# A new order of all steps in a sketched linear attention followed by a gated feed-forward layer

## The chip, the cores and the metric

The kernel runs on one core of a Trainium2 chip. A core has five engines with instruction streams of their own: TensorE (PE in the profile, its weight loads PEld), VectorE (DVE), ScalarE (ACT), GpSimd (POOL) and SyncE (SP, which here only issues transfers). Each engine runs its stream strictly in the order in which the program was written; an instruction that has to wait holds up everything behind it on its engine. The metric is the device time of one execution in microseconds.

## The reference

For 4 batches and 4 heads, 1088 tokens of 32 features each, queries and keys are turned into 64 products of two 8-wide projections; attention is linear in them. The result, laid out as 4352 tokens by 128, goes through a feed-forward layer of 2048 hidden units with a Swish whose slope is given for each unit.

```python
def phi(x):                                   # r = 8
    a = np.einsum('rd,bhsd->bhsr', S1, x)
    b = np.einsum('rd,bhsd->bhsr', S2, x)
    return np.einsum('bhsi,bhsj->bhsij', a, b).reshape(*x.shape[:-1], r * r)
q_p, k_p = (phi(q), phi(k))
kv = np.einsum('bhsf,bhsd->bhfd', k_p, v)
z = np.sum(k_p, axis=2)
num = np.einsum('bhsf,bhfd->bhsd', q_p, kv)
den = np.einsum('bhsf,bhf->bhs', q_p, z)[..., None] + 1e-06
x = (num / den)                               # then to (4352, 128)
h = x @ w_in
g = h * (1.0 / (1.0 + np.exp(-beta * h)))
return (g @ w_out).astype(np.float32)
```

## The kernel before

There is one list of short names, `SEQ`, and the program is written by calling the step of each name in turn. No scheduler reorders anything: the list is the order on every engine, and also the order in which buffers are handed out. A buffer that is used again makes its next writer wait for its last reader.

**The feed-forward part.** The tokens are cut into 9 chunks, eight of 512 and one of 256. A chunk has eight waves (the last has four). `W` (`first`, L433) is a wave's two matmuls of 512 columns (four of 256 in the last chunk) from xT, the attention's result, into a `wave` tile of PSUM; `G` (`silu`, L449) is one ScalarE instruction over the wave's 1024 columns; `V` (`second`, L400) is the wave's two matmuls into the output's accumulator; `E` (`put_out`, L414) transposes a finished chunk on VectorE and stores it. There are 68 waves, and two `wave` tiles. The scaled weights are made in the kernel: `up`/`uv` make 256 columns of winp on GpSimd or VectorE (L342), `wa`/`wp` make woutp on ScalarE or GpSimd (L351, L358). The slope beta is split in three bf16 parts (`bsv` on VectorE or `bsp` on GpSimd, L319 to L322), broadcast by TensorE (`be0`, `be1`, L327) and copied out by ScalarE (`bc0` to `bc3`, L337).

**The attention part, for a batch b.** `lk`, `lq`, `lv` issue its loads on SyncE. `tk`, `tq` transpose keys and queries on VectorE (L457, L463). `kp` projects the keys on TensorE (L475), `ka` transposes that on VectorE into kab (L489), and `op`/`ov` form products of the two projections, a piece at a time, on GpSimd or VectorE (L512, tile kp). `v` multiplies them with v on TensorE (L536). `z` sums the products on VectorE (L523), `zm` and `wz` carry the sums on into the tile sw. For batches 0 and 1 a shorter way takes their place: `gr` (L714, tile gram), `gd` (L734), `wm` (L760) and `wc` (L769). `qp` projects the queries together with the denominators (L596), `qa` transposes the two halves of the result (L608), `dp`, `di` and `as` form the denominators' reciprocals and scale one factor (L616, L626/L629, L634), `yp`/`yv` form the queries' products (L512, tile qo), `t` transposes them (L639, tile qt). `kd`, `np`, `nc` turn the key-value sums (L574, L577, L586, tile nd), `n` is the numerator on TensorE (L652), and `xa`/`xv` copy it to xT (L664).

**Batch 0's first 512 tokens** go a way of their own, so that the first waves can start early: `aA`, `bA`, `cA`, `mA` make their query products, `dA` and `iA` their denominators (iA: L786, L788, L789, L791 on VectorE), `kd0`, `nd0`, `nc0`, `nA` the numerator, and `xA` writes xT (L825 on VectorE).

**Buffers that matter here.** PSUM has two `wave` tiles (also used by `qp` and `n`), one `two` tile (`be`, `kp`, `qp`, `nd0`, `n` by turns) and one `one` tile (`gr`, `wm`, `np`, `v` of batches 1 to 3 and others by turns). The tiles kp, qo, qab and qt have one buffer each.

**Warming matmuls.** `h` is one matmul of 400 columns on constant data (L196) with no use for the result; it keeps TensorE busy. Six are issued ahead of the list.

SyncE's transfers use eight semaphores in turn, so that a transfer is issued only when the eighth before it has landed.

Of the kernel before, what the change touches and what calls it, by code (L numbers as in the profile page):

```python
# [18 lines left out]
SEQ = """
    lqA lq0 h li0 h li1 h lk1 sp lv0 bsv h h s0 h sw h s1 tk0b be0 sk h tk0a h bc0 h li2 h h bc1 tqA  # L20
    h sr lo1 kp0 tq0 src up0 h lk2 ka0a bA up1 ka0b aA ca0a lo0 ov04 gr0 op02 cA0 ov03 ov00 h op01 h
    be1 ztv op06 gdv0 lq1 tk1 bc2 h op05 h lv1 h ca0b zm cA1 op08 h mA0 bc3 h op07 v03 v05 mA1 wm0
    kp1 zc up3 wc0 v01 rb dA ka1 up2 v02 h h iA lo2 up7 v07 v08 v00 wa6 wa7 v04 up5 qp0 lq2 wa4 wa5
    v06 gr1 qa00 kd0 op13 kda0 qa01 nd0 h gdv1 h tk2 nc0 h lv3 h nA wa2 wa3 dpp0 wm1 h op10 wc1 h xA
    wa0 wa1 np0 h di0 nca0 W op12 W tq1 G kp2 asp0 h G W ov11 h v12 uv4 lo3 G W yv00 v13 G lv2 W ka2
    yp01 h v10 t00 G v11 qp1 up6 t01 kda1 W op22 wa10 wa11 qa11 h G V qa10 op23 lk3 W np1 lq3 tq2 n0
    G dpp1 ncv1 W ov21 xa01 V xa00 op20 di1 G W V G asp1 z20 W V wp4 G W yp13 V G W z21 v23 G W yp12
    v22 G W yp10 v21 t13 zm2 G W wz2 V yp11 G t10 W v20 t12 wa12 wa13 wp7 qp2 t11 G V qa20 V kda2
    qa21 n1 E0 dpv2 V di2 xa10 V W xv11 asp2 V G tk3 W yp22 V G W tq3 kp3 G W yv21 V G W yp20 ka3 V
    G W yp23 t20 V G V W E1 np2 op32 W G t21 V ncv2 V G ov31 W V op33 t22 G W t23 V G W op30 V G W  # L30
    v33 z30 G W V G n2 z31 v31 xa21 W V G W xv20 zm3 v30 G W wz3 V G qp3 E2 v32 qa31 W V qa30 G W V
    dpv3 G W di3 V G kdv3 W asp3 V G yp31 W V G W yp32 V G W yv33 V G V yp30 W E3 np3 W G t31 V ncv3
    V G t32 W V t30 G W t33 V G W V G V W V G W V G n3 E4 W xa31 V G xv30 W V G V W V G W V G W V G
    W V G W V G W E5 V G W V G W V G V W V G W V G W V G W V G W E6 V G W V G W V G W V G W V G W V
    G W V G V W E7 V G V V V E8
"""


# [919 lines left out]
```

## Time and profile before

| | before |
|---|---|
| median of 3 runs | 104.11 us (103.93 to 106.35) |
| the profiled execution's own time | 103.7 us |
| its span, first to last instruction | 101.9 us |
| PE, ACT, DVE, POOL busy | 96.3, 79.1, 64.0, 41.0 us |
| granted TensorE clock | 0.992 |
| first wave's matmuls start | 19.55 us |
| batch 3's numerator (last attention work on PE) | 73.96 to 75.50 us |
| last matmul of the chain ends | 98.1 us |
| DMA | 11.35 MB; the 16 engines are full until about 20 us |

The times in rows of the trace are microseconds from the span's start: a start, a duration, the engine, the line, the operation, output and input tiles, the number of instructions merged, and in brackets how long the engine had been idle and for whom. "x4" rows give the time from the first's start to the last's end.

### The profile page before, as it was taken

To read this page: it belongs to the slowest core of one execution; us is meant where nothing else is said; L and a number is where in the kernel's file an instruction comes from. 1 tells how busy PE (TensorE), PEld (TensorE's weight loads), DVE (VectorE), ACT (ScalarE), POOL (GpSimd) and SP (SyncE) were. 2 spreads that over 40 slices of the span, in tenths; PEclk is the share of its full clock that TensorE was granted. 3 is DMA by queue.
4 is the path that set the end of the run, shared out by engine and by line. 5 is a ranking of instruction groups with operands and counts; after the bars stand their busy time and mean duration, and the time that the engine had idled before them with its cause. 6 is when DMAs were issued, how large, how long until landed. Compare 5 with 4: busy or idle time off the path is not lost.

```text
span 101.9 us, 2974 instructions
## 1 busy us (share of the span) xinstructions
PE 96.3 (95%) x1225; PEld 48.4 (47%) x1225; DVE 64.0 (63%) x105; ACT 79.1 (78%) x110; POOL 41.0 (40%) x60
## 2 busy tenths in 40 slices
PE   5999999998999999999999999999999999999940
PEld 2465556435353454434544544454454444446730
DVE  2389989999999999995999578358032020020210
ACT  1553618699589995599997859999969999999920
POOL 7306998993976980499800001960000000000000
PEclk9999999999999999999999999999999999999996
DMA  1999999954738100330320000506012306014054
GB/s 29 306 264 385 415 398 378 358 176 149 214 71 330 68 6 0 60 52 0 57 46 6 0 9 10 90 0 103 0 19 31 60 6 100 0 24 71 8 88 67
DMA packets 23576, 11.35 MB, mean 111 GB/s; under 512 B 19323, under 2 KB 21387, under 8 KB 23563
## 3 DMA queue, kind: packets, MB, share of 16 engines
q1 hardware_dynamic: 22419, 11.08, 39.2%
q10 hardware_dynamic: 1144, 0.09, 0.8%
q8 instruction: 9, 0.15, 0.6%
q14 instruction: 4, 0.03, 0.1%
HBM read 8.94 MB, written 2.23 MB: 110 GB/s over the span
## 4 chain that ended last, share of the span: by engine, by line
PE 88%; DVE 7%; issue 0%
PE wave L433 30%; PE moeout L400 29%; PE kvz L196 8%; PE nps L652 6%; PE kvz L536 4%; PE qps L596 3%; PE kps L475 2%; DVE qo L512 1%; DVE winp L342 1%; DVE qT L463 1%; PE aps L684 1%; PE ndps L577 1%; DVE kp L512 1%; DVE kab L489 1%; PE gram L714 1%; PE kvz L714 1%
## 5 line engine op out<-in xcount | busy, mean ns | idle before, releaser
L449 ACT ACTIVATE g<-wave 128x1024 f16<-128x1024 f32 x68 | 64.8, 1036 | 4.8 <-PE wave L433 4.7
L433 PE MATMUL wave<-xT,winp 128*128 128x512 f16 (+1 forms) x144 | 40.6, 369 | 0.0
L400 PE MATMUL moeout<-g,woutp 128*128 128x512 f16 (+1 forms) x144 | 38.4, 367 | 0.1
L433 PEld LDWEIGHTS <-winp 128*128 128x128 f16 x144 | 15.2, 115 | 15.4 <-issue 5.3
L414 DVE STREAM_TRANSPOSE o_sb<-moeout 128x512 f32<-128x512 f32 (+1 forms) x9 | 6.1, 683 | 26.1 <-PE moeout L400 26.1
L400 PEld LDWEIGHTS <-woutp 128*128 128x128 f16 x144 | 13.8, 97 | 14.8 <-issue 0.8
L512 POOL TENSOR_TENSOR kp<-kab 128x256 f32<-128x256 f32 (+2 forms) x15 | 14.3, 976 | 1.9 <-DVE kab L489 1.6
L512 POOL TENSOR_TENSOR qo<-qab 128x512 f32<-128x512 f32 (+1 forms) x11 | 13.9, 1295 | 0.2
L196 PE MATMUL kvz<-idle 128*128 128x400 f16 x40 | 10.8, 381 | 1.2 <-DVE idle L115 1.1
L639 DVE STREAM_TRANSPOSE qt<-qo 128x512 f32<-128x512 f32 (+1 forms) x14 | 10.1, 753 | 0.0
L634 POOL TENSOR_TENSOR qab<-qab,rc 128x288 f32<-128x288 f32 (+1 forms) x4 | 2.5, 632 | 18.7 <-DVE rc L629 18.7
L523 DVE TENSOR_REDUCE zs<-kp 128x128 f32<-128x1152 f32 x4 | 8.4, 2145 | 0.0
L536 PEld LDWEIGHTS kvz<-kp,v 128*32 128x32 f32 x288 | 4.9, 109 | 5.7 <-issue 3.9
L536 PE MATMUL kvz<-kp,v 128*32 128x64 f32 x288 | 7.3, 224 | 0.0
L342 POOL TENSOR_TENSOR winp<-w_in_sb,beta_bc 128x256 f16<-128x256 f32 x7 | 5.1, 753 | 5.2 <-DMA w_in_sb<-in_moe_w_in_dram 5.2
L196 PEld LDWEIGHTS <-idle 128*128 128x128 f16 x40 | 3.8, 109 | 4.7 <-issue 2.5
L652 PE MATMUL nps<-qt,nd 32*32 32x288 f32 (+1 forms) x256 | 6.0, 386 | 0.0
L664 ACT CAST xT<-nps 128x576 f16<-128x576 f32 (+1 forms) x5 | 2.8, 553 | 3.7 <-PE nps L652 3.6
L463 DVE STREAM_TRANSPOSE qT<-q 128x1088 f32<-128x1088 f32 (+2 forms) x5 | 5.2, 1047 | 0.4 <-DMA q<-in_q_dram 0.4
L457 DVE STREAM_TRANSPOSE kT<-k 128x1088 f32<-128x1088 f32 (+2 forms) x5 | 5.4, 1074 | 0.0
L608 DVE STREAM_TRANSPOSE qab<-qps 128x576 f32<-128x576 f32 (+1 forms) x8 | 5.2, 683 | 0.3 <-PE qps L596 0.2
L351 ACT ACTIVATE woutp<-w_out_sb,rbeta 128x128 f16<-128x128 f32 x12 | 4.1, 396 | 1.6 <-DMA w_out_sb<-in_moe_w_out_dram 1.6
(102 smaller groups left out, 71.1 us busy)
## 6 DMA issues: line engine op xcount, KB each, us to landing
v<-in_v_dram SPq DMA_DIRECT2D x15, 144.0 KB, 5.7
k<-in_k_dram SPq DMA_DIRECT2D x3, 544.0 KB, 6.5
q<-in_q_dram SPq DMA_DIRECT2D x3, 544.0 KB, 7.5
out_dram<-o_sb SPq DMA_DIRECT2D x20, 64.0 KB, 2.0
w_out_sb<-in_moe_w_out_dram SPq DMA_DIRECT2D x4, 256.0 KB, 6.6
w_in_sb<-in_moe_w_in_dram SPq DMA_DIRECT2D x2, 256.0 KB
w_in_sb<-in_moe_w_in_dram SPq DMA_DIRECT2D x1, 512.0 KB
k<-in_k_dram SPq DMA_DIRECT2D x1, 288.0 KB, 2.8
```

The source lines that it names most:

```text
L196: nc.tensor.matmul(out=kvz0[:, HC : HC + 400], lhsT=idle, rhs=cut(idle, [[0, 25], [1, 16]]), start=fresh, stop=True, skip_group_check=True,)
L342: eng.tensor_tensor(out=winp[:, c0:c1], in0=w_in_sb[:, c0:c1], in1=beta_bc[:, c0:c1], op=MUL)
L400: nc.tensor.matmul(out=moe["acc"][:, :tw], lhsT=woutp[:, j, :], rhs=g[jj], start=(j == 0), stop=(j == NJ - 1),)
L414: nc.vector.transpose(out=o_sb[:, :nt, :].rearrange("p t d -> p (t d)"), in_=PS["acc", ci][:, :tw])
L433: nc.tensor.matmul(out=wv[:, jj // per, o : o + tw], lhsT=cut(winp, [[step, P]], c), rhs=xT[:, t0 : t0 + tw], start=True, stop=True,)
L449: nc.scalar.activation(out=g, in_=wv, func=ACTF.Silu)
L463: nc.vector.transpose(out=qT2[b % 2][:, t0:t1].rearrange("p t s -> p (t s)"), in_=q_t[b][:, t0:t1].rearrange("p t d -> p (t d)"),)
L512: eng.tensor_tensor(out=cut(dst[b][:, j0:j1], [[F, n], [R, R], [1, R]]), in0=left, in1=cut(a0, [[w, n], [0, R], [1, R]], o + R), op=MUL,)
L523: nc.vector.tensor_reduce(out=RB["zs", b][:, hs].rearrange("p h f -> p (h f)"), in_=KP[b][:, :, hs].rearrange("p j h f -> p (h f) j"), axi ...
L536: nc.tensor.matmul(out=KVZ[b][32 * h : 32 * h + 32, :F], lhsT=v_t[b][:, h, j, :], rhs=KP[b][:, j, h, :], start=(b > 0 and summed[b] == 0), ...
L639: nc.vector.transpose(out=QT[b][:, j0:j1].rearrange("p j h c s -> p (j h c s)"), in_=QO[b][:, j0:j1].rearrange("p j h f -> p (j h f)"),)
L652: nc.tensor.matmul(out=ts[g // 2][32 * h : 32 * h + 32, g % 2, : 32 * nq], lhsT=ND[b][rows, fc, 32 * h : 32 * h + 32], rhs=QT[b][rows, :nq ...
```

## The change

Only the list `SEQ` differs: 473 names in place of 474. The same work is done. Two warming matmuls fall away (32 `h` in place of 34). Some steps change the engine: the split of beta goes from VectorE to GpSimd; the denominators' products go from GpSimd to VectorE for batches 0 and 1 and from VectorE to GpSimd for batches 2 and 3; the scaling for batch 3 goes to VectorE; all of batch 0's query products are on GpSimd; batch 3 has two pieces of key products and two of query products on VectorE in place of one each; ScalarE takes two more pieces of woutp (14 in place of 12) and one more copy each to nd and xT. All else is order. The first two lines of the list, as an example:

```diff
-    lqA lq0 h li0 h li1 h lk1 sp lv0 bsv h h s0 h sw h s1 tk0b be0 sk h tk0a h bc0 h li2 h h bc1 tqA
-    h sr lo1 kp0 tq0 src up0 h lk2 ka0a bA up1 ka0b aA ca0a lo0 ov04 gr0 op02 cA0 ov03 ov00 h op01 h
+    lqA lk1 h lv0 h h h sp tk0a h bsp h h h li1 tk0b h lq0 sk li0 s1 kp0 s0 sw lk2 sr ka0b h h src
+    ka0a h op07 ca0b h h tqA ca0a be0 op06 ov04 lo1 gr0 bc0 op01 li2 rb aA bc1 ov05 lo0 op00 bA ztv
...
```

On VectorE, from the transposed key projections of batch 1 (kab) to the first write of xT, the order was this (dps, rc and rb are the denominators of the first 512 tokens, qab the query projections of batch 0, gd a part of batch 1's gram matrix, kT batch 2's keys):

```order
L489 STREAM_TRANSPOSE kab<-kps 128x2x9x32 [waits PE_49]
L786 STREAM_TRANSPOSE dps<-dps 128x256 [waits DVE_49,PE_49,Activation_49]
L788 TENSOR_SCALAR rc_355<-dps 128x16 [waits DVE_49]
L789 RECIPROCAL rc_355<-rc_355 128x16 [waits DVE_49]
L791 STREAM_TRANSPOSE rb<-rc_355 128x512 [waits DVE_49]
L608 STREAM_TRANSPOSE qab<-qps 128x2x5x32 [waits PE_49] x2
L734 TENSOR_TENSOR gd_429<-gram,mh 128x32 [waits PE_49]
L457 STREAM_TRANSPOSE kT_112<-k 128x1088 [waits DMAHW1_49]
L825 TENSOR_TENSOR xT<-nps,rb 128x512 [waits DVE_49,PE_49]
```

On the same engine, between the same two steps, it is now:

```order
L489 STREAM_TRANSPOSE kab<-kps 128x2x9x32 [waits PE_49]
L457 STREAM_TRANSPOSE kT_112<-k 128x1088 [waits DMAHW7_49]
L512 TENSOR_TENSOR kp<-kab 128x512 [waits DVE_49,PE_49,Pool_49]
L608 STREAM_TRANSPOSE qab<-qps 128x2x5x32 [waits PE_49]
L786 STREAM_TRANSPOSE dps<-dps 128x256 [waits PE_49,Activation_49]
L788 TENSOR_SCALAR rc_403<-dps 128x16 [waits DVE_49]
L789 RECIPROCAL rc_403<-rc_403 128x16 [waits DVE_49]
L791 STREAM_TRANSPOSE rb<-rc_403 128x512 [waits DVE_49]
L608 STREAM_TRANSPOSE qab<-qps 128x2x5x32
L825 TENSOR_TENSOR xT<-nps,rb 128x512 [waits DVE_49,PE_49]
```

Batch 2's keys, a piece of batch 1's key products and half of qab now stand ahead of the denominators, and gd no longer stands here.

On ScalarE, around the first waves, the order was this (nd is batch 0's turned key-value sums, g a wave's result; the numbers tell the buffers apart):

```order
L769 COPY sw1_117<-w_457 128x8 [waits PE_49]
L351 ACTIVATE woutp_148<-w_out_sb_90,rbeta_149 128x128 x2
L586 COPY nd_476<-ndps_469 128x256 [waits PE_49]
L449 ACTIVATE g_486<-wave_478 128x1024 [waits PE_49]
L449 ACTIVATE g_499<-wave_482 128x1024 [waits PE_49]
```

On ScalarE, at the same place, it is now:

```order
L351 ACTIVATE woutp_148<-w_out_sb_90,rbeta_149 128x128 x3
L449 ACTIVATE g_460<-wave_449 128x1024 [waits PE_49]
L586 COPY nd_463<-ndps_444 128x256
L449 ACTIVATE g_465<-wave_457 128x1024 [waits PE_49]
L449 ACTIVATE g_489<-wave_479 128x1024 [waits PE_49]
L449 ACTIVATE g_516<-wave_486 128x1024 [waits PE_49]
L769 COPY sw1_117<-w_511 128x8 [waits PE_49]
```

The copy to nd, which empties the `one` tile, has moved behind the first wave's silu, and the copy to sw1 behind the fourth. On TensorE the gram matrix of batch 1 (`gr1`, which writes the `one` tile next) has moved from ahead of the first wave to behind the second; then come two waves, batch 2's key projections, `wm1`, and two more waves.

On VectorE, behind the first write of xT, the order was this (dpr feeds batch 0's denominators, qT are the transposed queries of batches 1 and 2):

```order
L626 TENSOR_REDUCE rc<-dpr_114 128x20 [waits Pool_49]
L629 RECIPROCAL rc<-rc 128x20 [waits DVE_49]
L463 STREAM_TRANSPOSE qT_115<-q 128x1088 [waits DMAHW3_49]
L512 TENSOR_TENSOR kp<-kab 128x512
L342 TENSOR_TENSOR winp<-w_in_sb,beta_bc 128x256 [waits DMAHW7_49]
L512 TENSOR_TENSOR qo<-qab 128x768 [waits Pool_49]
L489 STREAM_TRANSPOSE kab<-kps 128x2x9x32 [waits PE_49]
```

On the same engine and at the same place, it is now:

```order
L616 TENSOR_TENSOR dpr_114<-qab 128x20x8 [waits DVE_49]
L342 TENSOR_TENSOR winp<-w_in_sb,beta_bc 128x256 [waits DMAHW1_49]
L626 TENSOR_REDUCE rc<-dpr_114 128x20 [waits DVE_49]
L629 RECIPROCAL rc<-rc 128x20 [waits DVE_49]
L463 STREAM_TRANSPOSE qT_111<-q 128x1088 [waits DMAHW3_49]
L463 STREAM_TRANSPOSE qT_115<-q 128x1088 [waits DMAHW4_49]
L734 TENSOR_TENSOR gd_491<-gram,mh 128x32 [waits PE_49]
L489 STREAM_TRANSPOSE kab<-kps 128x2x9x32 [waits PE_49]
```

Both batches' queries are now transposed ahead of gd and of batch 2's kab, and the products of keys and of queries that stood here are on GpSimd or further ahead. From batch 3's numerator to the end the two lists name the same steps with the same number of waves left: 22 `W`, 22 `G`, 28 `V`.

More of the change, by code (lines that the diff above doesn't have):

```diff
@@ L19 @@
 SEQ = """
-    lqA lq0 h li0 h li1 h lk1 sp lv0 bsv h h s0 h sw h s1 tk0b be0 sk h tk0a h bc0 h li2 h h bc1 tqA
-    h sr lo1 kp0 tq0 src up0 h lk2 ka0a bA up1 ka0b aA ca0a lo0 ov04 gr0 op02 cA0 ov03 ov00 h op01 h
-    be1 ztv op06 gdv0 lq1 tk1 bc2 h op05 h lv1 h ca0b zm cA1 op08 h mA0 bc3 h op07 v03 v05 mA1 wm0
-    kp1 zc up3 wc0 v01 rb dA ka1 up2 v02 h h iA lo2 up7 v07 v08 v00 wa6 wa7 v04 up5 qp0 lq2 wa4 wa5
-    v06 gr1 qa00 kd0 op13 kda0 qa01 nd0 h gdv1 h tk2 nc0 h lv3 h nA wa2 wa3 dpp0 wm1 h op10 wc1 h xA
@@ L25 @@
[L25 to L34, printed above, removed]
@@ L35 @@
-    G W V G V W E7 V G V V V E8
+    lqA lk1 h lv0 h h h sp tk0a h bsp h h h li1 tk0b h lq0 sk li0 s1 kp0 s0 sw lk2 sr ka0b h h src
+    ka0a h op07 ca0b h h tqA ca0a be0 op06 ov04 lo1 gr0 bc0 op01 li2 rb aA bc1 ov05 lo0 op00 bA ztv
+    lq2 tk1 op03 h cA1 v00 lq1 h be1 cA0 up2 mA1 lo3 h v03 bc2 op08 h v04 mA0 bc3 h lv1 up3 ov02 kp1
+    gdv0 up1 tq0 v08 v02 v06 v01 ka1 wm0 h wc0 v05 zm tk2 h v07 kd0 ov10 zc qp0 kda0 dA up0 qa00 iA
+    nd0 h h lo2 nc0 h wa4 wa5 h h nA wa2 wa3 lv2 qa01 h h wa0 wa1 xA h h np0 dpv0 h W uv5 op13 di0 W
@@ new lines @@
+    G tq2 nca0 G op12 gr1 tq1 W up7 h lq3 W G gdv1 up6 kp2 lv3 wm1 G up4 ka2 op11 W wc1 W G V asp0
+    v13 yp01 G lk3 qp1 v10 wa8 wa9 v11 yp00 t01 V wa6 wa7 V W v12 qa11 G qa10 wa14 wa15 t00 kda1
+    wa10 wa11 dpv1 n0 ov21 di1 op20 W xa01 V xa00 op22 G np1 V W op23 nca1 W G V wp6 G z20 asp1 V V
+    yp10 W W z21 G v20 yp13 v23 G W v22 G yp12 t10 zm2 W E0 G yp11 t13 V V wz2 W t12 qp2 G t11 V
+    qa20 v21 V qa21 n1 dpp2 di2 W xa11 V xa10 kdv2 V asp2 tk3 G W V G np2 yv22 W V yp20 G W E1 kp3 G
+    yp21 t22 W ka3 V G yp23 W t21 G t20 W V op31 G t23 W V G ncv2 op32 W V G W ov30 V ov33 G W V G
@@ L36 @@
+    z31 V W V G W v33 z30 G v30 v31 W n2 G E2 zm3 tq3 W xa21 V G W wz3 V G xv20 W V G W V G qp3 v32
+    qa31 W kda3 V qa30 G W V dpp3 G W V di3 G W asv3 V G W yp33 E3 np3 G W V G yv30 W V yv32 G W
+    yp31 t33 V G W V t31 G W t32 V G t30 W V ncv3 G W V G W V G n3 E4 W xa31 V G xv30 W V G V W V G
+    W V G W V G W V G W V G W E5 V G W V G W V G V W V G W V G W V G W V G W E6 V G W V G W V G W V
+    G W V G W V G V W V G W E7 V G V V V E8
 """
```

## The prediction

> **What bounds the kernel now.** First the busy times and the chain that ended last, then the stages, then single rows.
>
> ```profile
> PE 96.3 (95%) x1225; PEld 48.4 (47%) x1225; DVE 64.0 (63%) x105; ACT 79.1 (78%) x110; POOL 41.0 (40%) x60
> PE wave L433 30%; PE moeout L400 29%; PE kvz L196 8%; PE nps L652 6%; PE kvz L536 4%; PE qps L596 3%; PE kps L475 2%; DVE qo L512 1%; DVE winp L342 1%; DVE qT L463 1%; PE aps L684 1%; PE ndps L577 1%; DVE kp L512 1%; DVE kab L489 1%; PE gram L714 1%; PE kvz L714 1%
> L196 PE MATMUL kvz<-idle 128*128 128x400 f16 x40 | 10.8, 381 | 1.2 <-DVE idle L115 1.1
> ```
>
> TensorE is the bound, and 8% of the chain is warming matmuls: filler, which marks where TensorE waits for others. The stages, cut at the first wave and at the ends of the numerators (columns: stretch, length, then busy PE, PEld, DVE, ACT, POOL, the clock, DMA):
>
> ```profile
> 19.55:29.31 9.76, 9.22 (x208) 4.39 (x207) 9.73 (x13) 8.21 (x12) 7.85 (x9) 1.00 0.55 172
> 29.31:41.18 11.87, 11.85 (x209) 5.28 (x210) 11.59 (x17) 10.17 (x14) 6.98 (x8) 1.00 0.30 98
> 41.18:56.15 14.97, 14.97 (x164) 7.05 (x168) 13.72 (x16) 13.02 (x14) 8.25 (x7) 1.00 0.24 38
> 56.15:75.56 19.41, 19.41 (x225) 9.33 (x226) 10.86 (x19) 16.81 (x18) 4.58 (x4) 1.00 0.18 28
> 75.56:98.13 22.57, 22.53 (x117) 11.89 (x116) 2.91 (x5) 21.20 (x23) 0.00 (x0) 1.00 0.25 39
> ```
>
> Until 41 us **VectorE is as full as TensorE** (9.73 of 9.76, 11.59 of 11.87), so what is put ahead of a critical step there delays it by its full length. From 41 to 75 us TensorE has no gap. In the tail ScalarE is nearly full too: 21.20 of 22.57.
>
> So the test of a new order is this: at equal TensorE work done (so many waves, `V`s and attention steps), is the clock earlier or later than before? I add it up at three points, from rows of before. A wave's two matmuls, and a `V`'s, count 0.43 us there, as in this piece of the chain:
>
> ```profile
> 42.15 0.43 PE wave L433 x2
> ```
>
> **The first wave.** It needs the first write of xT, on VectorE.
>
> ```profile
> 12.15 0.60 ACT L337 COPY beta_bc<-betaps 128x512 f32<-128x512 f32 x1
> 13.95 0.78 DVE L489 STREAM_TRANSPOSE kab<-kps 128x576 f32<-128x576 f32 x1 [0.33 <-PE kps L475]
> 14.65 0.46 DVE L786 STREAM_TRANSPOSE dps<-dps 128x256 f32<-128x256 f32 x1
> 16.28 0.87 DVE L608 STREAM_TRANSPOSE qab<-qps 128x320 f32<-128x320 f32 x2
> 17.26 1.30 DVE L457 STREAM_TRANSPOSE kT<-k 128x1088 f32<-128x1088 f32 x1
> 18.75 0.69 DVE L825 TENSOR_TENSOR xT<-nps,rb 128x512 f16<-128x512 f32 x1 [0.19 <-PE nps L814]
> 19.36 0.33 DVE L626 TENSOR_REDUCE rc<-dpr 128x20 f32<-128x180 f32 x1
> 21.09 0.82 DVE L512 TENSOR_TENSOR kp<-kab 128x512 f32<-128x512 f32 x1
> 21.84 1.28 DVE L342 TENSOR_TENSOR winp<-w_in_sb,beta_bc 128x256 f16<-128x256 f32 x1
> ```
>
> Before, xT waited 0.19 us for TensorE. Now VectorE does kab, kT, kp, half of qab, the denominators, the other half, xT. By starts to next starts: 0.70 + 1.25 + 0.75 + 1.63 + 0.87 = 5.20 us (kT's 1.30 less 0.05 of overlap). Batch 0's keys are projected earlier now, because the split of beta has left VectorE. But batch 1's projections still wait for the last copy of beta, since both use the tile `two`, and I leave kab at 13.95. xT then starts at 19.15, and the first wave at about 19.95: **0.4 us later**. (TensorE's own way there, from half of qab over nd0, nc0 and nA past the `h`s, ends at about the same time.) What was gained on the keys is hidden.
>
> The keys and queries must also have landed. Each transfer waits for the eighth before it, so an issue dates a landing:
>
> ```profile
> 8.50 0.33 SPq L172 DMA_DIRECT2D w_out_sb<-in_moe_w_out_dram  x1
> 10.69 0.33 SPq L172 DMA_DIRECT2D w_out_sb<-in_moe_w_out_dram  x1
> 15.24 0.33 SPq L172 DMA_DIRECT2D w_out_sb<-in_moe_w_out_dram  x1
> 16.60 0.33 SPq L122 DMA_DIRECT2D q<-in_q_dram  x1
> ```
>
> The transfers eight ahead of these end 1344, 2144, 3488 and 4032 KB of the old queue. In the new one batch 2's keys end 3264 KB, so about 14.5 us, and their transpose starts at 14.65: just in time. Batch 2's and 1's queries end 4832 and 5376 KB; at the 319 KB/us between the second and the last row that is 19.1 and 20.8 us, and their transposes start after 21.5.
>
> **From there to batch 0's numerator.**
>
> ```profile
> 19.55 1.03 PE L433 MATMUL wave<-xT,winp 128*128 128x512 f16 x4
> 20.51 0.71 PE L475 MATMUL kps<-kT,sk 64*32 64x288 f32 x16
> 19.58 0.37 ACT L586 COPY nd<-ndps 128x256 f32<-128x256 f32 x1
> 20.18 4.92 ACT L449 ACTIVATE g<-wave 128x1024 f16<-128x1024 f32 x5 [0.23 <-PE wave L433]
> 19.91 1.25 DVE L463 STREAM_TRANSPOSE qT<-q 128x1088 f32<-128x1088 f32 x1
> 26.61 1.40 DVE L608 STREAM_TRANSPOSE qab<-qps 128x576 f32<-128x576 f32 x2
> 28.13 1.17 PE L652 MATMUL nps<-qt,nd 32*32 32x160 f32 x64
> ```
>
> TensorE has two waves issued 0.96 us after the first starts (19.55 to 20.51). Then `gr1` needs the tile `one`, which ScalarE's copy to nd empties, and this copy is now behind a silu: the silu starts 0.63 us after the first wave (20.18), 0.96 us on the next thing can start (4.92 us for five), and the copy takes 0.37. So TensorE **stands about 1.0 us**, from 20.9 to 21.9. What is queued behind: gram, all waves, batch 2's keys. The gram and `wm1` (0.8 us) were done before the first wave in the old order, while four `h`s that ran behind it are gone (about 0.8 us in all). Then TensorE has gram to 22.6, two waves and an `h` to 23.7, batch 2's projections to 24.35, and `wm1`, which needs gd. VectorE reaches gd behind xT, the denominators' product (0.3, an estimate from its size beside the reduce), winp (1.2), reduce and reciprocal (0.55) and two transposes of queries (1.25 each): 19.76 + 4.55 = 24.3. So wm1 loses only a little, to 24.5. After it come two waves, a `V`, kv products and the query projections of batch 1, to 27.0. The numerator needs their two transposes (1.40) and that of 768 columns of batch 0's products (0.9, an estimate by the row at 35.29, quoted below): 29.3, while TensorE has work until 28.85. It ends at 30.4. Before, it ended at 29.31 with the same 7 waves, but one `V` in place of three and batch 1's ndps (0.22) done already. At equal work: 30.4 - 0.86 + 0.22 - 29.31 = **0.45 us late**. "Four waves ahead of its queries" thus fills time that the order itself opens.
>
> **To batch 1's numerator.** VectorE sums batch 2's key products, which GpSimd makes.
>
> ```profile
> L512 POOL TENSOR_TENSOR kp<-kab 128x512 f32<-128x512 f32 x6 | 6.4, 1068 | 1.6 <-DVE kab L489 1.6
> L512 POOL TENSOR_TENSOR kp<-kab 128x768 f32<-128x768 f32 x3 | 4.5, 1509 | 0.3 <-POOL winp L342 0.3
> 31.18 4.21 DVE L523 TENSOR_REDUCE zs<-kp 128x128 f32<-128x1152 f32 x2
> 35.29 0.98 DVE L639 STREAM_TRANSPOSE qt<-qo 128x768 f32<-128x768 f32 x1
> 36.65 1.89 DVE L639 STREAM_TRANSPOSE qt<-qo 128x512 f32<-128x512 f32 x3
> 38.72 1.45 DVE L608 STREAM_TRANSPOSE qab<-qps 128x576 f32<-128x576 f32 x2 [0.18 <-PE qps L596]
> 39.58 1.60 PE L652 MATMUL nps<-qt,nd 32*32 32x288 f32 x64
> ```
>
> The tile kp is free when batch 1's last kv product is done, at 28.85. Three pieces (1.07 + 1.07 + 1.51) end at 32.5, the two sums at 36.8. Then VectorE has four transposes of qt, one output of the same size as qt's of 512 (0.6), the two small steps of `wz` (0.4, between the rows at 35.29 and 36.65) and qab: 0.96 + 1.89 + 0.6 + 0.4 + 1.4 = 5.2 us, so 42.0. TensorE runs out of `V`s at 41.4, stands 0.6 us, and ends the numerator at 43.5 with 15 waves and 12 `V`s; before 41.18, with 16 and 8. 43.5 - 3 x 0.43 - 41.18 = **1.0 us late**.
>
> **The rest.** The order is nearly the old one, and VectorE has room again. ScalarE has one more xT copy there (about 0.64) and kvd (0.37), and fewer finished waves in store at 43.5 us (3 for 8), so that TensorE waits for it more often. From nothing to those 1.0 us; I take 0.2, because ScalarE had 1.95 us idle in that stage and 2.6 in the next. The tail has the same steps. What hides the two more woutp pieces (0.35 each) on ScalarE is its wait for TensorE before batch 0's numerator; without that they push the eighth silu back by 0.7.
>
> **Sum.** 0.45 + 0.55 + 0.2 = 1.2 us. The profiled execution took 103.7, the median of the runs is 104.11; on the median, **105.3 us** (+1.2%).
>
> **The shared port.** Products on VectorE and GpSimd at once:
>
> ```profile
> 49.68 1.39 DVE L512 TENSOR_TENSOR kp<-kab 128x512 f32<-128x512 f32 x1
> 46.96 3.56 POOL L512 TENSOR_TENSOR kp<-kab 128x512 f32<-128x512 f32 x3
> 44.98 0.65 DVE L512 TENSOR_TENSOR qo<-qab 128x512 f32<-128x512 f32 x1
> 42.95 4.05 POOL L512 TENSOR_TENSOR qo<-qab 128x512 f32<-128x512 f32 x3
> ```
>
> The same size took VectorE 1.39 us, 0.82 and 0.65, the last beside GpSimd for its whole length. The Trainium skill, "GPSIMD Engine Reference", section "Key points", says that GpSimd shares its SBUF interfaces with VectorE and contends with its instructions of two SBUF inputs. By that rule each such pair is slow; the trace bears it out in the first row and not in the third.
>
> **Rivals.** (1) *Slower by more*: the new order puts the product on kab and GpSimd's 768-column piece of the same batch side by side ahead of the first wave, as both start when batch 0's kv is done. At 1.39 in place of 0.75 the first wave loses 0.6 more, and the pieces of batch 2 ahead of the sums as much again; with 0.3 for a late landing of batch 2's keys, 106.8 us. For it speaks the full VectorE, against it the 0.65. Chance 0.17. (2) *No effect*: TensorE's work is fixed, and the waits replace filler: the stand of 1.0 us is paid by the four `h`s, VectorE's order is made good by waves done ahead. 104.1, chance 0.15. (3) *Not slower*: if batch 1's projections start at once after the last copy of beta (12.75 before) with kab at 13.4, and TensorE's way to nA runs early because the keys are early, the first wave comes at 19.4 to 19.5, batch 0's numerator is level, and the sums of batch 2 start early enough that TensorE never stands at batch 1's: then the 1.0 us of the two stands turns into filler saved, 103.1. It decides at the start of VectorE's kab: before about 13.4 it is this case. Chance 0.15. That the waves aren't ahead at all, because winp's pieces are late on GpSimd (1.51 + 1.07 and three pieces of winp at no more than 1.28 each, from batch 0's last kv product at about 15, end by 21.4; the wave comes at 24.5), is within (1).
>
> **How the numbers follow.** The forecast has 0.53, for 104.5 to 106.1. The range 103.2 to 107.1 leaves out about half of (3) and a third of (1). 2% is about what a measurement of this kernel can tell from no change: 102.0 and 106.2 are its bounds. Faster takes a little of (3), 0.03; slower most of (1) and the forecast's upper edge, 0.19; the rest, 0.78, is within.
>
> **What would show it.** First wave near 19.95 with VectorE, not nps, ending last before it; TensorE idle near 1 us behind the second wave, released by the nd copy; batch 0's numerator waiting for qt or qab; batch 1's end near 43.5 behind zs; from batch 3's numerator on the same distances. If the first wave is ahead of 19.5 or the sums of batch 2 start before 32, I am wrong towards (3).

## The result, and the profile after

The changed kernel takes **107.4 us** (106.68 to 107.81 in four runs), the kernel before 104.4 beside it: 1.030 times, interval 1.021 to 1.038. The forecast was 105.3 with a range to 107.1: the direction was right, the loss 3.0 us in place of 1.2. The profiled execution took 107.16 us, with a span of 105.4. Executions that were disturbed are left out of all ratios and of the run times in the table below; the profiled executions of e4, e8, e9, e13, e17 and e19 are among them, and of these only the distances behind the first wave are compared.

The busy times of the changed kernel, and its stages, cut at the same events as before (first wave, ends of the four numerators, end of the last matmul):

```profile
PE 97.7 (93%) x1223; PEld 48.7 (46%) x1223; DVE 63.8 (61%) x101; ACT 79.9 (76%) x114; POOL 41.3 (39%) x61
...
19.91:31.31 11.40, 10.03 (x233) 5.14 (x232) 8.92 (x14) 9.14 (x17) 6.83 (x9) 1.00 0.68 224
31.31:44.95 13.64, 12.71 (x214) 5.78 (x214) 11.04 (x15) 9.28 (x14) 9.51 (x9) 1.00 0.15 28
44.95:60.62 15.67, 15.42 (x195) 7.31 (x198) 15.11 (x17) 14.46 (x16) 6.75 (x6) 1.00 0.12 20
60.62:79.06 18.44, 18.33 (x190) 8.50 (x190) 11.12 (x17) 16.80 (x19) 3.78 (x3) 1.00 0.18 29
79.06:101.58 22.52, 22.52 (x117) 11.90 (x116) 2.91 (x4) 21.20 (x23) 0.00 (x0) 1.00 0.25 39
```

The clock is 1.00 in all five stretches, as it was before, so nothing of the loss behind the first wave is the clock's. TensorE stands 1.37 and 0.93 us in the first two of these stretches (10.03 busy of 11.40, 12.71 of 13.64), where it stood 0.54 and 0.02 before, and VectorE, once full there, waits too: at times each waits for the other, as the brackets below show. The tail is as long as before.

Single rows of the timeline of the changed kernel, in the order of time:

```profile
13.73 0.74 DVE L489 STREAM_TRANSPOSE kab<-kps 128x576 f32<-128x576 f32 x1
15.91 0.69 DVE L512 TENSOR_TENSOR kp<-kab 128x512 f32<-128x512 f32 x1 [0.24 <-PE kvz L536]
15.95 3.04 POOL L512 TENSOR_TENSOR kp<-kab 128x768 f32<-128x768 f32 x2 [2.00 <-PE kvz L536]
17.17 0.47 DVE L786 STREAM_TRANSPOSE dps<-dps 128x256 f32<-128x256 f32 x1
19.20 0.65 DVE L825 TENSOR_TENSOR xT<-nps,rb 128x512 f16<-128x512 f32 x1
19.91 1.02 PE L433 MATMUL wave<-xT,winp 128*128 128x512 f16 x4
21.45 0.37 ACT L586 COPY nd<-ndps 128x256 f32<-128x256 f32 x1
21.87 0.77 PE L714 MATMUL gram<-kab 128*64 128x32 f32 x18 [0.94 <-ACT nd L586]
26.65 0.78 PE L596 MATMUL qps<-qT,sw 32*32 32x288 f32 x32
27.70 1.45 DVE L608 STREAM_TRANSPOSE qab<-qps 128x576 f32<-128x576 f32 x2 [1.78 <-PE qps L596]
29.89 4.33 POOL L512 TENSOR_TENSOR kp<-kab 128x512 f32<-128x512 f32 x3 [4.36 <-PE kvz L536]
30.15 1.16 PE L652 MATMUL nps<-qt,nd 32*32 32x160 f32 x64 [0.37 <-DVE qt L639]
30.27 1.56 DVE L512 TENSOR_TENSOR kp<-kab 128x512 f32<-128x512 f32 x1
34.25 4.31 DVE L523 TENSOR_REDUCE zs<-kp 128x128 f32<-128x1152 f32 x2 [1.62 <-POOL kp L512]
43.35 1.60 PE L652 MATMUL nps<-qt,nd 32*32 32x288 f32 x64
44.99 1.31 ACT L664 CAST xT<-nps 128x576 f16<-128x576 f32 x2 [2.65 <-PE nps L652]
46.20 12.53 ACT L449 ACTIVATE g<-wave 128x1024 f16<-128x1024 f32 x13
```

The first wave comes at 19.91 and TensorE stands 0.94 us for the copy to nd, both as forecast. Batch 0's numerator ends at 31.3 in place of the forecast 30.4; GpSimd's pieces of batch 2 start 1.0 later than forecast (29.89 for 28.85) and take 4.33 us in place of 3.65, with VectorE's piece beside them at 1.56; batch 1's numerator ends at 44.95 in place of 43.5. Behind it ScalarE, idle for 2.65 us before, works without a gap until 58.7.

Where the 3.45 us at the last matmul went (101.58 against 98.13), at equal TensorE work (0.43 per wave or `V`, 0.22 for `np1`, about 0.5 for 28 to 32 kv matmuls of batch 3 that stand on the other side of a cut, from the 0.92 us that 56 of them take):

| stretch | longer by | at equal work | forecast |
|---|---|---|---|
| to the first wave | 0.36 | 0.36 | 0.4 |
| to batch 0's numerator | 1.66 | 1.00 | 0.05 |
| to batch 1's | 1.75 | 1.10 | 0.55 |
| to batch 2's | 0.71 | 0.64 | 0.2 with the next |
| to batch 3's | -0.99 | 0.37 | |
| tail | 0.0 | 0.0 | 0 |

### The profile page after: what moved, and what is told of

Same layout as the page of the kernel before. It is cut to its first block, busy times and chain, and to the rows that moved or that the text cites. A ratio compares the mean times of both kernels' runs of the same rounds, so it can differ in the third digit from the quotient of the medians.

```text
span 105.4 us, 2966 instructions
## 1 busy us (share of the span) xinstructions
PE 97.7 (93%) x1223; PEld 48.7 (46%) x1223; DVE 63.8 (61%) x101; ACT 79.9 (76%) x114; POOL 41.3 (39%) x61
## 4 chain that ended last, share of the span: by engine, by line
PE 78%; ACT 7%; DVE 5%; POOL 5%; issue 1%; DVEq 0%; ACTq 0%
PE moeout L400 25%; PE wave L433 25%; PE kvz L196 9%; ACT g L449 7%; PE kvz L536 5%; PE nps L652 4%; POOL kp L512 4%; DVE zs L523 2%; PE qps L596 2%; PE kps L475 2%; DVE o_sb L414 1%; PE aps L684 1%; PE betaps L327 1%; PE ndps L577 1%; PE gram L714 1%
## 5 line engine op out<-in xcount | busy, mean ns | idle before, releaser
L616 POOL TENSOR_TENSOR dpr<-qab 128x288 f32<-128x288 f32 x2 | 1.6, 792 | 17.8 <-DVE qab L608 17.8
L664 ACT CAST xT<-nps 128x576 f16<-128x576 f32 (+1 forms) x6 | 3.4, 566 | 4.0 <-PE nps L652 4.0
```

## The experiments

Two properties of the order make small differences readable. The list is fixed, so a stage that an edit doesn't touch mostly repeats to a few hundredths of a microsecond; and most of what varies between executions lies ahead of the first wave (the exceptions, in the first stage of e9, e10 and e13, are told of below). So beside the run times (which carry that variation) the starts of the first wave and of the four numerators are compared in each profiled execution:

| kernel | run times, us | first wave | to n0 | n0 to n1 | n1 to n2 | n2 to n3 | n3 to end |
|---|---|---|---|---|---|---|---|
| before | 103.9 to 104.7 | 19.55 | 8.58 | 11.45 | 14.96 | 19.42 | 27.94 |
| changed | 106.7 to 107.8 | 19.91 | 10.24 | 13.20 | 15.67 | 18.43 | 27.95 |
| e5, nd copy first | 106.3, 107.0 | 19.95 | 9.39 | 13.17 | 15.68 | 18.43 | 27.88 |
| e3, last kv piece early | 106.2 to 107.2 | 20.11 | 10.25 | 12.23 | 15.67 | 18.44 | 27.90 |
| e11, both | 105.5 to 106.1 | 20.12 | 9.39 | 12.20 | 15.68 | 18.43 | 27.88 |
| e6, xT first | 108.3 to 109.3 | 20.08 | 11.74 | 13.19 | 15.67 | 18.43 | 27.89 |
| e16, all pieces on GpSimd | 107.8 to 109.2 | 19.95 | 10.25 | 13.75 | 15.67 | 18.44 | 27.94 |
| e12, VectorE late by a hair | 108.6, 109.2 | 21.95 | 10.25 | 13.18 | 15.67 | 18.43 | 27.92 |
| e7, pairs in the tail | 109.4 | 22.20 | 10.25 | 13.18 | 15.67 | 18.43 | 27.97 |
| e1, old head, new rest | 105.6 to 106.1 | 20.07 | 8.57 | 11.45 | 16.48 | 19.78 | 27.95 |
| e4, copies on VectorE | 107.3, 108.0 | 22.41 | 10.25 | 13.18 | 15.75 | 18.44 | 27.97 |
| e8, a wave ahead | 108.8 to 109.1 | 22.20 | 10.25 | 13.76 | 15.95 | 18.43 | 28.71 |
| e10, a silu ahead | 107.7 to 108.8 | 21.38 | 10.51 | 13.20 | 15.58 | 18.39 | 27.94 |
| e9, e3 with e5 and e8 | 106.8 to 107.4 | 21.48 | 10.50 | 12.82 | 15.94 | 18.44 | 28.72 |
| e13, e11 with e10 | 105.5 to 105.9 | 21.55 | 10.41 | 12.22 | 15.58 | 18.38 | 27.86 |
| e14, idle copy | 107.5 to 108.2 | 19.80 | 10.25 | 13.17 | 16.14 | 18.44 | 27.90 |
| e15, idle copy, before | 104.1 to 105.2 | 20.65 | 8.58 | 11.44 | 15.33 | 19.42 | 27.98 |
| e17, less for ScalarE | 107.6, 108.7 | 22.23 | 10.25 | 13.18 | 15.54 | 18.43 | 27.87 |
| e19, and its waves first | 107.6, 109.1 | 22.38 | 10.26 | 13.16 | 15.77 | 18.43 | 27.90 |

(The late first waves of e4, e7, e8, e17 and e19 are told of under e12, those of e9, e10 and e13 in the last section.) The first theory (A) put the whole loss ahead of batch 1's numerator. Its rivals were the new rest of the list (B), TensorE that only swaps a `V` for a wait, so that an earlier chain elsewhere gains little (C), and a later wait, for gd, that covers the stand (D).

**The stand behind the first silu (e5).**

```diff
- xA h h np0 dpv0 h W uv5 op13 di0 W G tq2 nca0 G
+ xA h h np0 nca0 dpv0 h W uv5 op13 di0 W G tq2 G
```

> The new order with ScalarE's copy to nd put back ahead of the first silu, so that the gram matrix finds its tile free. By my prediction's term (TensorE stands 1.0 us there): the stand of 0.94 us goes and the kernel gains about 1.0, 106.4. Theory D (the step behind it, wm1, waits for VectorE's gd behind two transposes of queries until 23.9 anyway): the stand goes, wm1 still starts near 24.0 to 24.4, and at most 0.4 us are gained, 107.0 or more.

```profile
19.92 0.37 ACT L586 COPY nd<-ndps 128x256 f32<-128x256 f32 x1 [0.43 <-PE ndps L577]
20.91 0.77 PE L714 MATMUL gram<-kab 128*64 128x32 f32 x18
29.34 1.20 PE L652 MATMUL nps<-qt,nd 32*32 32x160 f32 x64 [0.38 <-DVE qt L639]
```

Gram now starts 0.96 us earlier with no wait, the way to batch 0's numerator is 0.85 us shorter, and all of it arrives at the end. The ratio to the kernel before is 1.025 (1.019 to 1.031). So the stand was real, and of its 0.94 us 0.85 was not covered by a later wait; D falls for this execution.

**The last kv piece (e3), and both edits (e11).**

```diff
- v11 yp00 t01 V wa6 wa7 V W v12 qa11
+ v11 v12 yp00 t01 V wa6 wa7 V W qa11
```

> One step of the new order is moved: batch 1's last kv product (v12) goes ahead of two V and a wave, so that the tile kp is free earlier for batch 2's products on GpSimd. Theory A (GpSimd's products of batch 2 start late and hold VectorE's sums, these hold batch 1's numerator, and after it ScalarE sets the pace, so that every gain there reaches the end): products start near 28.5 in place of 29.9, sums near 32.9 in place of 34.25, batch 1's numerator ends near 43.6 in place of 44.9, and the kernel takes 106.0 us. Theory C (work done ahead counts: TensorE only swaps a V for a wait): no more than 0.4 us gained, 106.9 or more.

> The edits of e3 (last kv piece early) and e5 (copy to nd ahead of the first silu) together, nothing else. If the stand behind gram and the late chain of batch 2's key products are two losses: 0.83 + 0.75 = 1.6 us faster than the changed kernel, 105.6 to 106.0 us, batch 1's numerator near 41.8 us. Rival: one hides behind the other: 106.3 to 106.6 us, the numerator no earlier than 42.5 us.

In e3, GpSimd and VectorE:

```profile
28.56 3.78 POOL L512 TENSOR_TENSOR kp<-kab 128x512 f32<-128x512 f32 x3 [3.08 <-PE kvz L536]
33.62 4.18 DVE L523 TENSOR_REDUCE zs<-kp 128x128 f32<-128x1152 f32 x2
```

The key products of batch 2 wait for batch 1's last kv piece, which stood behind two `V`s and a wave. With it ahead of those, the pieces start 1.33 us earlier and the stage is 0.97 us shorter (1.024, interval 1.020 to 1.029); C, which allowed 0.4, falls. It isn't the whole 1.33 because the sums no longer wait for GpSimd: VectorE itself gets to them only 1.3 us after the pieces are done, and its own piece beside them now takes 2.00 us in place of 1.56. Together (e11) the two edits give 0.85 and 1.00, as if alone: 105.8 us in the middle, 1.017 (1.012 to 1.022). Of the 2.1 us between the first wave and batch 1's numerator this accounts for 1.85.

**Does the first wave's start count (e6)?** `tk2` and `ov10` go behind `xA`.

> Batch 2's key transpose and batch 1's one key product on VectorE go behind the first write of xT: the first wave can start up to 2.0 us earlier, at 18 to 18.6 us. If the first wave's start counts one for one (the prediction's first term), the kernel ends 1 us or more earlier than the changed one: 106.3 us or less. Rival: what VectorE does up to gd is the same in sum and wm1, batch 1's queries and batch 2's sums come when they came, so TensorE only stands elsewhere: within 0.4 us of the changed kernel.

```profile
16.52 0.52 DVE L608 STREAM_TRANSPOSE qab<-qps 128x320 f32<-128x320 f32 x1 [2.15 <-PE qps L596]
17.35 0.47 DVE L786 STREAM_TRANSPOSE dps<-dps 128x256 f32<-128x256 f32 x1 [0.32 <-PE dps L775]
18.27 0.66 PE L814 MATMUL nps<-qp,nd 64*32 64x256 f32 x16
19.38 0.65 DVE L825 TENSOR_TENSOR xT<-nps,rb 128x512 f16<-128x512 f32 x1
26.05 0.15 DVE L734 TENSOR_TENSOR gd<-gram,mh 128x32 f32<-128x32 f32 x1
26.25 0.25 PE L760 MATMUL w<-gd,srep 128*32 128x8 f32 x8 [1.63 <-DVE gd L734]
```

Neither expectation was met. The wave did not come earlier at all: without the two steps VectorE stands 2.15 us for TensorE's query projections and 0.32 for its dps matmuls, and starts its transpose of dps at 17.35, in the changed kernel at 17.17. From there to the first wave it is 2.73 us here and 2.74 there. It is not nps that holds xT: nps ends at 18.93 and xT starts at 19.38. Ahead of xT the two steps had filled a wait and cost nothing; behind it 2 us more of VectorE stand between xT and gd, so that gd comes 2.3 us later, TensorE stands 1.63 us for it, and the kernel is slower still, 1.044 (1.037 to 1.050).

**VectorE and GpSimd exclude each other (e7, e16, e12).** e7 adds products on dead data in the tail, e16 moves VectorE's piece of batch 2 (`ov21` becomes `op21`), and e12 puts a copy of four columns ahead of `ov10`.

> The changed kernel with extra products on data that nobody needs any more, in the tail. Behind the last write of xT: two products of 512 columns on VectorE alone, then two of 768 on GpSimd alone. Behind the sixth output: three of 768 on GpSimd and five of 512 on VectorE, started together. Behind the seventh: three of 768 on GpSimd and six transposes of 1024 columns on VectorE. Alone about 0.62 and 1.51 each. Lock theory (whoever starts first holds the shared port for its whole instruction, the other waits): the pair's total is the sum, three GpSimd pieces take about 1.51 + 0.62 each where VectorE comes between (6 us together in place of 4.5) and a VectorE product 0.62 plus up to a whole GpSimd piece (up to 2.1); transposes at once without any loss. Rival (the two share the port at a lower rate): every VectorE product is lengthened by the same factor, about 1.39/0.65 = 2.1, and GpSimd too. Rival (no shared port; the long rows came from waits): 0.62 and 1.51 side by side.

In e7 (prv and prp are the dead targets), alone, then the pair (columns of the two lines with "x5" and "x3": shortest, median and longest in ns, first and last start), then transposes beside GpSimd:

```profile
82.72 1.41 DVE L845 TENSOR_TENSOR prv<-kab 128x512 f32<-128x512 f32 x2
84.42 3.09 POOL L845 TENSOR_TENSOR prp<-kab 128x768 f32<-128x768 f32 x2
...
L845 DVE TENSOR_TENSOR prv<-kab x5: 683/1879/2025, 88.8 to 95.4; 128x512 f32<-128x512 f32 x5
L845 POOL TENSOR_TENSOR prp<-kab x3: 1503/1834/1840, 89.5 to 93.0; 128x768 f32<-128x768 f32 x3
...
96.68 4.43 DVE L880 STREAM_TRANSPOSE prv<-kab 128x512 f32<-128x512 f32 x6
96.97 4.68 POOL L845 TENSOR_TENSOR prp<-kab 128x768 f32<-128x768 f32 x3
```

Side by side the two take turns: a VectorE product that alone takes 0.69 us takes 1.88 to 2.03, that is a whole GpSimd piece and then itself, and each GpSimd piece after the first waits for a VectorE product. The first of each kind, and VectorE's last, when the other was done, have their own length. Three pieces and five products, 4.5 and 3.4 us alone, end after 7.3 us, so that only 0.6 us of the 7.9 overlap. Transposes lose nothing. That is a lock and not a sharing of speed, which would have lengthened every product by the same factor. The Trainium skill states it in "SBUF — State Buffer", section "SBUF: two separate sides": the pair is an exclusive lock, whoever starts first has it for its whole instruction. These rows agree.

> In the changed kernel the one piece of batch 2's key products that VectorE makes goes to GpSimd, so that GpSimd makes all four. Lock theory: VectorE's piece held the port for its length and saved GpSimd little: GpSimd's chain goes from 4.33 us for three pieces to about 4.7 for four, batch 2's sums start 0.2 to 0.5 us later, and the kernel is 0 to 0.5 us longer. Rival (each engine works at its own speed): the sums start 1.0 us later and the kernel is about 1 us longer, as that wait is on the way to batch 1's numerator.

```profile
29.94 4.91 POOL L512 TENSOR_TENSOR kp<-kab 128x512 f32<-128x512 f32 x4 [4.44 <-PE kvz L536]
34.88 4.28 DVE L523 TENSOR_REDUCE zs<-kp 128x128 f32<-128x1152 f32 x2 [3.55 <-POOL kp L512]
```

VectorE's piece had taken only 0.58 us off GpSimd's chain (4.91 against 4.33) for a piece that takes GpSimd 1.05; the stage is 0.55 longer, between the two expectations and nearer the lock's.

> A copy of four columns on VectorE (about 0.15 us) that waits for the same buffer, directly ahead of the product of batch 1's keys that VectorE makes beside GpSimd before the first wave; the product overwrites what it copies. In the changed kernel's profile VectorE starts that product at 15.91 and GpSimd its piece of 768 columns at 15.95. Lock theory: now GpSimd starts first, VectorE's product takes about 1.9 us in place of 0.69, TensorE stands more than 1 us ahead of ndps, and the first wave comes 1.3 us late or more, at 21.2 us or later. If a stand of that length also lowers the granted clock, as in two disturbed runs (0.50 for 3 us), the whole is 2.0 to 2.4 us longer: 109.2 to 109.8 us. Rival (no lock): 0.15 us longer at most, 107.6 us or less, the product 0.7 us.

```profile
16.63 2.98 POOL L513 TENSOR_TENSOR kp<-kab 128x768 f32<-128x768 f32 x2 [1.85 <-PE kvz L537]
16.79 1.90 DVE L513 TENSOR_TENSOR kp<-kab 128x512 f32<-128x512 f32 x1
```

In the changed kernel's profile VectorE began this product 0.04 us ahead of GpSimd's piece. With a copy in front it comes 0.16 us behind and takes 1.90 us in place of 0.69. From GpSimd's start to the first wave it is 5.32 us in place of 3.96: 1.36 later. The rest of the late first wave (21.95) arose ahead of these rows: GpSimd's piece itself starts 0.68 later. By the medians the kernel is 1.5 us slower than the changed one (1.046, interval 1.040 to 1.053); the clock did not fall here.

The same happens without the copy when batch 2's keys land late. The order of e7's head is the changed kernel's (the last row is a stretch of 1 us: busy PE, PEld, DVE, ACT, POOL, then the clock):

```profile
14.32 1.31 DVE L458 STREAM_TRANSPOSE kT<-k 128x1088 f32<-128x1088 f32 x1 [0.34 <-DMA k<-in_k_dram]
15.46 2.98 POOL L513 TENSOR_TENSOR kp<-kab 128x768 f32<-128x768 f32 x2 [1.48 <-PE kvz L537]
15.56 1.96 DVE L513 TENSOR_TENSOR kp<-kab 128x512 f32<-128x512 f32 x1
18.00 0.48 PE L578 MATMUL ndps<-ident,kvd 128*128 128x128 f32 x1 [1.45 <-DVE qab L609]
18.00:19.00 1.00, 1.00 (x4) 0.58 (x5) 0.90 (x4) 0.49 (x3) 1.00 (x2) 0.50 1.07 384
```

**The rest of the list (e1, e4, e8, e10, e9, e13).** e1 has the old order up to batch 1's numerator and the new one behind it; e4 gives one copy to xT and one to kvd back to VectorE; e8 puts the last wave of chunk 1 ahead of `qp2` for a `V` behind `n1`; e10 puts it between `qp2` and `n1`. The core of e10:

```diff
- qp2 G t11 V qa20 v21 V qa21 n1 dpp2 di2 W xa11 V xa10 kdv2 V
+ qp2 G t11 V qa20 v21 W qa21 G n1 dpp2 di2 V xa10 V xa11 W kdv2 V
```

> The old order up to and with batch 1's numerator, then the new order of the rest. Theory A (all of the loss arises ahead of the end of batch 1's numerator, the rest is as good as before): 104.1 to 104.8 us, numerator of batch 3 ends near 75.6. Theory B (about 1 us is lost by the new rest itself, by its additional ScalarE copies and its other engines for products): 105.2 us or more, numerator of batch 1 at 41.2 as before, of batch 3 at 76.6 or later.

> The new order with two copies put back from ScalarE to VectorE: the second xT copy of batch 1 and batch 3's kvd. If ScalarE sets the pace behind batch 1's numerator (theory A): 0.6 to 1.0 us gained, 106.4 to 106.8, and the first silu behind that numerator starts near 45.6 in place of 46.2. If TensorE sets it (theory C): no change, 107.2 to 107.4.

> The last wave of chunk 1 goes ahead of batch 1's query projections and numerator, in place of a V, which goes behind; the waves behind it are each one ahead. Theory B2: from batch 1's numerator on ScalarE sets the pace (silus at 0.92 us, back to back), so what counts there is the number of finished silus, and this one falls into ScalarE's 2.65 us wait: 0.9 to 1.3 us faster than the changed kernel, 106.1 to 106.5 us, the numerator itself within 0.2 us of 43.35, and the distance from its end to the end of batch 3's numerator 33.2 or less in place of 34.1. Rival (equal TensorE work, as in the prediction: a wave for a V is worth nothing): within 0.3 us of the changed kernel.

> The last wave of chunk 1 goes between batch 1's query projections and its numerator (so it takes no wave tile from the projections), one V goes behind the numerator for it, and the wave ahead of batch 2's numerator goes behind that one, so that from there on the list is the changed one with the same work done. Theory B3: between the two numerators ScalarE sets the pace of the changed kernel (from 44.99 to 58.73 us two xT copies and 13 silus without a gap), and one silu fewer there shortens that stage by 0.6 to 0.9 us, less 0.2 us for a numerator that waits for batch 1's second half of qab: 0.3 to 0.7 us faster than the changed kernel, 106.6 to 107.0 us, batch 2's numerator ahead of 58.7 us. Rival (equal TensorE work, it waits for nothing there): within 0.2 us.

e1 repeats the old head (8.57, 11.45) and then needs 36.26 us from batch 1's to batch 3's numerator where the kernel before needs 34.38: the new rest costs up to 1.9 us with the old head ahead of it, though the place where the two orders are joined (three `V`s on end, a copy that ScalarE makes in another order) is part of that. A falls as the whole cause; it holds for the part ahead of the numerator. e4 wins nothing: the second wave starts at 48.92, when the copy on VectorE ends (48.12, 0.76 us long), since it takes over the numerator's wave tile. e8 lost 0.56 ahead of the numerator, where the projections waited for a wave tile, 0.28 in the next stage and 0.76 in the tail, where one wave fewer is left; the cause in the tail was not tested. e10 avoids that and wins 0.09 and 0.04.

> The edits of e3 (last kv piece early), e5 (copy to nd ahead of the first silu) and e8 (a wave for a V ahead of batch 1's numerator) together. If the three causes are apart, the gains add: 0.75 + 0.83 + 0.9 to 1.3 = 2.5 to 2.9 us, so 104.5 to 104.9 us, about 0.5 us from the kernel before. Rival: one wait hides behind the other, so that together they give no more than the largest two: 105.6 to 106.3 us.

> The edits of e10 and e11 together. If the three losses are apart: 0.83 + 0.75 + what e10 gains alone (0.3 to 0.7) faster than the changed kernel, 105.0 to 105.5 us; what then is left beyond the kernel before is the later first wave (0.36 us) and the rest of the way to batch 0's and 1's numerators. Rival: with the numerator 1.6 us earlier ScalarE's wait ahead of it is gone, so that the early silu gains nothing: 105.6 to 106.0 us.

e9 (e3, e5 and e8) can't be told from the changed kernel by its ratio, 1.026 (1.020 to 1.031): e8's losses of 0.56, 0.28 and 0.76 return in its stages. e13 (e11 with e10) takes 105.5 to 105.9 us, 1.014 (1.008 to 1.020), its rival's figure: not to be told from e11, and still behind the kernel before. In the profiled executions of both, e5's gain is gone again (10.50 and 10.41 in the table for e11's 9.39): `dpv0` and `uv5`, on VectorE ahead of gd, took 0.71 and 1.28 us in e13 where they took 0.30 and 0.41 in e11, and TensorE stood for gd. There D holds, and whether e5's edit pays depends on that start. The row is e13's:

```profile
26.38 0.25 PE L760 MATMUL w<-gd,srep 128*32 128x8 f32 x8 [0.98 <-DVE gd L734]
```

**Is it ScalarE (e14, e15, e17, e19)?** An idle copy of 0.57 us on ScalarE behind batch 1's numerator in the changed kernel (e14) and in the kernel before (e15); then (e17) half of batch 1's xT left out (zeros from GpSimd) and a silu cut to 16 columns; then (e19) the waves moved ahead of the `V`s as well. In e17 and e19 part of batch 1's result is not computed.

> The changed kernel with one idle copy on ScalarE (576 columns, as long as a copy to xT, about 0.65 us) behind the first silu that follows batch 1's numerator; nothing reads it. If from there to batch 2's numerator ScalarE sets the pace (13 silus without a gap), TensorE has too few finished silus in store to do anything else, and the kernel is 0.5 to 0.7 us longer: 107.9 to 108.1 us, batch 2's numerator 0.5 us or more later against batch 1's. Rival (TensorE's own work or VectorE sets it): within 0.2 us of the changed kernel.

> The same idle copy in the kernel before, behind the first silu that follows batch 1's numerator. There 16 waves with their silus are done at that point and 8 V's, so TensorE has 8 finished silus in store, and ScalarE is idle for 1.95 us of the stage: within 0.2 us of the kernel before. Rival (ScalarE's silus pace every order at this place): 0.5 us longer or more.

> The changed kernel with less for ScalarE behind batch 1's numerator: one of its two copies to xT is left out (the tokens are zero instead, written by GpSimd while it is idle), and the first silu behind it covers 16 of its 1024 columns (the rest is zero). That is what ScalarE has more there than in the kernel before: one copy of 0.64 and one silu of 0.92 us, less about 0.2 us for the small one. If this is what the order loses from batch 1's numerator on, the way from that numerator's end to the end of batch 3's goes from 34.1 to 33.1 us or less (33.1 is the kernel before at equal TensorE work), and the kernel takes 106.2 to 106.5 us. Rival (ScalarE is only a part of it, as the idle copy's 0.47 of 0.57 us and the silu moved ahead, worth 0.1, together leave open): 33.5 to 33.9 us.

> As the run with less for ScalarE (one copy to xT and most of one silu left out), and the two V's that stood between the first and the second wave behind batch 1's numerator go behind the second, so that ScalarE, now free earlier, also gets its waves earlier; the wave ahead of batch 2's numerator goes behind it, so that the same work is done there. In the run with less work alone ScalarE stood 1.05 us for that second wave. If the two together, work on ScalarE and the place of its waves, make up the microsecond, the way from the end of batch 1's numerator to the end of batch 3's is 33.1 to 33.5 us in place of 33.97 (34.11 in the changed kernel). Rival (the loss in that stretch is not ScalarE's): 33.8 us or more.

```profile
47.92 0.18 ACT L851 ACTIVATE g<-wave 128x16 f16<-128x16 f32 x1
49.16 9.67 ACT L449 ACTIVATE g<-wave 128x1024 f16<-128x1024 f32 x10 [1.05 <-PE wave L433]
```

The copy costs 0.47 us of its 0.57 in the changed kernel and 0.37 in the kernel before: ScalarE is on the way in both, and more finished silus in store protect the old order only a little. But with 1.23 us less for ScalarE in the stage (e17, the rows above; 13.23 us busy in place of 14.46) only 0.13 is won: it then stands 1.05 us for a wave that the list has behind two `V`s. With the waves first (e19) the stage is 15.77, no better; ScalarE still stands 0.55 and 0.44 us for waves there, and TensorE 0.25 for a silu. TensorE and ScalarE go in step over two wave tiles, and relief of the one shows the other's wait. So the last 1.0 us lies between batch 1's and batch 3's numerators, ScalarE's extra copy and silu are on its way, but no single edit won it back: its cause is left open.

## Why the prediction was right or wrong

The direction was right. All three terms of the sum, 0.45, 0.55 and 0.2 us, were too small: at equal TensorE work they came out as 1.36, 1.12 and 1.0.

- **What bounds the kernel, and the tail.** Right: the tail is 27.95 us from the last numerator's start, 27.94 before, and each edit ahead of it arrives in full at the end.
- **The first wave.** Right in size (19.91 for 19.95), and VectorE did end last ahead of it, not nps. But the cause was wrong, so the size was luck in part: not VectorE's added 1.25 + 0.75 us set it but TensorE's own way to dps, for which VectorE's chain waits; e6 took the 2.0 us away and won nothing.
- **The stand of 1.0 us.** Right (0.94; worth 0.85 in e5). The step that failed is what followed, "30.4": the numerator ended at 31.3. The query projections ended 0.36 later than summed, at 27.36 (two waves and a `V` ahead of them took about 0.55 each in place of 0.43), VectorE began 0.34 after their end, and TensorE 0.15 after VectorE's three transposes, which took 2.3 as summed. Thus 1.36 late at equal work in place of 0.45, mis-sized by a chain summed without its handovers.
- **Batch 2's key products, "(1.07 + 1.07 + 1.51) end at 32.5".** Mechanism right, size wrong twice: the tile came free 1.0 us later, since the kv piece behind two `V`s and a wave was dated too early, and three pieces took 4.33 us beside VectorE's piece and another product of VectorE's, which by the lock hold GpSimd up. The stage lost 1.12 in place of 0.55; e3 gives 0.97 of it back.
- **"I take 0.2", of "nothing to those 1.0".** Mis-sized: 1.0 at equal work (34.10 us from batch 1's to batch 3's numerator, for 34.38 less three `V`s of 0.43 before), the upper end. ScalarE's work is on the way there; what makes up the 1.0 stays open.
- **The shared port.** The rule was right and the reading "not in the third row" was wrong: VectorE's 0.65 had started first, at 44.98, and GpSimd paid. In the kernel before, this piece of 768 columns took 2.00 us in place of 1.51:

```profile
45.00 2.00 POOL L512 TENSOR_TENSOR qo<-qab 128x768 f32<-128x768 f32 x1
```

- **Rival (1)** named both places of the port and a late landing of batch 2's keys; at batch 2's pieces it came true in the profiled run, ahead of the first wave only in other executions (22.2 us in e7's). Its 106.8 was nearer than the forecast. **Rival (2)** fell: filler paid next to nothing (and of its four `h`s one still stands behind the first wave). **Rival (3)** fell: VectorE's kab came at 13.73, not ahead of the 13.4 from which it was to hold. In e5 and e11 kab did come ahead of that, at 13.34 and 13.28, and the first wave still came at 19.95 and 20.12, so that sign alone did not decide.

## What to carry to other kernels

In a fixed order, date each step from the last thing queued ahead of it on its engine, handovers included: two steps that stood one place too late (a copy behind a silu, a matmul piece behind two others) made 1.85 of the 3.45 us by which the last matmul ends later (101.58 for 98.13), added up when cured together, and were each cured by moving one name. And before a step is moved off a busy engine, see whether it fills a wait there: ahead of xT two steps of 2.0 us cost nothing. Look for two-input products that VectorE and GpSimd start at the same event: the order of a few hundredths of a microsecond decides which one waits out the other's whole instruction, so give one of them a place of its own. Compare edits by the distances between fixed events in the profile: behind batch 0's numerator they repeated to 0.03 us in stages that the edit left alone, where run times scattered by 1.
